# Attention and feed-forward on one core: the second layer's block products regrouped into 512-column steps, its blocks and sums in one tile, and transfers in flight counted by the planner

## The chip, the cores and the metric

One NeuronCore of a Trainium2 chip runs the whole program in one launch. The metric is the device time of one execution in microseconds; lower is better. Engines: TensorE (PE, with PEld for its weight loads), VectorE (DVE), ScalarE (ACT), GpSimd (POOL) and SyncE (SP, which here issues most DMAs).

## The reference

Causal attention with a decay, 8 batches of 8 heads, 576 positions, head size 64; its output, 4608 tokens of 512, goes through two matrix products with a leaky Relu between them. All is float32.

```python
scores = scale * np.matmul(q, k.transpose(0, 1, 3, 2))
cum = np.cumsum(np.log(np.clip(f, 0.0001, 1.0)), axis=-1)
scores = np.where(causal, -1000000000.0, scores + cum[:, :, :, None] - cum[:, :, None, :])
attn = np.exp(scores - np.max(scores, axis=-1, keepdims=True))
attn = attn / (np.sum(attn, axis=-1, keepdims=True) + 1e-09)
x = np.matmul(attn, v).transpose(0, 2, 1, 3).reshape(B * S, H * D)
h = x @ w_in                                       # 512 -> 2048, "first layer"
g = np.maximum(h, 0.0) + alpha * np.minimum(h, 0.0)
return g @ w_out                                   # 2048 -> 512, "second layer"
```

## The kernel before

**Arithmetic.** A float32 product is made of three fast ones: each operand is split into a high part (a copy in the fast format, by ACT) and a low part (the operand less its high part, by DVE or POOL), and high x high, high x low and low x high are added up in PSUM. A PSUM bank is 128 x 512 floats; there are eight.

**Attention and first layer.** 32 pairs of heads follow one another. From pair 9 on (`turned`) the exponentials are turned over by DVE transposes and by 16 small moves a pair of 100 KB (line 920), which SP and POOL issue in turns. The sums' reciprocals go out to DRAM and come back spread over the partitions (`fetch`, lines 657 and 1000); for the last of the first four pairs (`hurry`) `quick` spreads them with six PE products instead. Line 979 or 982 multiplies the attention output by them, 988 and 989 split it. Then the first layer (`ffn1`) can use it: for each of nine token blocks `b` and 16 slices `fc` of its output, twelve matmuls of 512 columns (line 364, `xx` and `wi`) fill one bank. ACT and DVE apply the leaky Relu (lines 1032, 1035, 1037) into one of three buffers `hs`, and SP stores it to DRAM as `hd` (line 1039, 256 KB), from DRAM position [slice][half][partition][token], 512 tokens on end. For the blocks in `LATE` (0, 7 and 8) the Relu is left to the second layer.

**Second layer** (`ffn2`). 18 units of 256 tokens, in the order `UNITS`. The product of a unit is cut into blocks of 128 tokens and 256 outputs, and done with seven block products in place of eight, on sums of blocks (four sums of the tokens' blocks A, four of the weights' blocks B made once in `load_w_out`). The 2048 inputs are taken as eight chunks of two halves, two chunks (`GW`) at a time: a group. For a group, SP loads `hd` into `hr` (line 1252, 512 KB), in late units ACT and DVE apply the Relu (1262, 1267), DVE makes the sums in `gx` (lines 1272 to 1275), ACT makes three pieces of high parts (line 1288) and DVE three of low parts (line 1291) in `gh`. Then PE does, for each of the two chunks, seven products of three matmuls of 256 columns (line 364, `gh` and `wot`): first three of them, then four, into four banks that the unit takes all at once. `PRODS` lists a product's A, its B, its bank and its half of it. After the last group ACT copies one half of bank 3 (line 1314) and DVE adds up the rest in four operations (lines 1318, 1319, 1322, 1323), and SP stores the output (line 1354). The last unit has its own, finer end.

**What sets the order.** Nothing is ordered by hand. Every operation is told to a planner (`Plan`, line 96) with its engine, an estimated duration, a key, the operations that it needs and the buffers that it uses (rings of tiles or banks). `Plan.run` goes through simulated time: of the operations that could start it takes the earliest, with the lower key at a tie, and emits it. So each engine's instructions stand in the planned order, and on the chip each engine works through its own in that order and waits on semaphores. While the plan's time is under 75 us, PE's idle stretches are filled with dummy matmuls (`fill`, line 466). The rings `rhr` (two tiles at first), `rgx` (one) and `rgh` (two) get more tiles when old ones come free: `change3` adds the scratch of the weight sums as four `hr`, `change5` the attention's `xs` as a second `gx`, `change2` the first layer's `xx` as a third `gh` (which the profile names `xx`). `c_mm`, `c_dve` and so on are the durations that the planner believes.

Of the kernel before, what the change touches and what calls it, by code (L numbers as in the profile page):

```python
# [91 lines left out]
ENGS = ("PE", "ACT", "DVE", "POOL", "SP", "-")  # L92


class Plan:
    def __init__(self):
        self.now = dict.fromkeys(ENGS, 0.0)
        self.chan = 0.0
        self.ops = []
        self.banks = self.fill = None  # L100
        self.rnd = random.Random(SEED)
# [27 lines left out]
    def run(self):  # L129
# [76 lines left out]
def attention_moe(  # L206
# [23 lines left out]
    hd = dram.tile([NW, 2, 128, NT], F32, name="hd")  # L230
# [14 lines left out]
    xx = xp.tile([128, 6 * 2 * 512], F32R, name="xx")  # L245
# [11 lines left out]
    hs = xp.tile([128, 7 * 256], F32, name="hs")  # L257
# [29 lines left out]
    xs = xp.tile([128, 2 * S], F32, name="xs")  # L287
    rxs = Ring(Store([xs[:, S * i : S * i + S] for i in range(2)]))
    rri = ring(xp, 1, [128, 4, 6, 32], F32, "ri")
# [6 lines left out]
    tri = sp.tile([128, 128], BF16, name="tri")  # L296
    tri2 = sp.tile([128, 64], BF16, name="tri2")
# [29 lines left out]
    def c_dve(n):  # L327
        return 75 + n / 0.96

# [215 lines left out]
    def attention(n):  # L545
# [4 lines left out]
        hurry = HURRY if n == NP - 1 else 0  # L550

# [75 lines left out]
        def quick(bR, r_, key):  # L627

            bB = [Buf(rT), Buf(rT)]
            at = lambda c0: bB[c0 // 512].t[:, c0 % 512 : c0 % 512 + (128 if c0 < 512 else 64)]  # L630
# [10 lines left out]
            for c0, c1 in ((0, 512), (512, S)):  # L641
                ri_ops.append(op("DVE", c_dve(c1 - c0), lambda c0=c0, c1=c1: ve.tensor_copy(flat(bri)[:, c0:c1], bB[c0 // 512].t[:, 0 : c1 - c0]), key, [q_], [bB[c0 // 512], bri]))

        def quotients(key):
# [8 lines left out]
            if hurry:  # L653
                quick(bR, r_, key)
# [108 lines left out]
        def rest():  # L763
            st = k0 + 11.5 - hurry
# [30 lines left out]
        quotients(k0 + 11 - hurry)  # L795
# [10 lines left out]
    def turned(n):  # L806
# [208 lines left out]
    def ffn1(b):  # L1015

        for fc in range(NF):
# [16 lines left out]
            else:  # L1034
# [5 lines left out]
                hd[fc % NW, fc // NW, :, 512 * b : 512 * b + 512], bs.t), -1000, [cp], [bs], kb=256)  # L1040
# [79 lines left out]
    rhr = ring_later(2, [128, GW, 2, TU], F32, "hr")  # L1120
    rgx = ring_later(1, [128, 4, GW, 128], F32, "gx")
# [20 lines left out]

    def change3():
        st = rhr.store
        for i in range(4):
            st.free.append((plan.t, len(st.items)))
            st.items.append(wx[0].rearrange("p a (b c j) n -> p (a b) c j n", b=2, c=GW)[:, i])

    def change2():
        n = 2 * 7 * GW * 128  # L1150
        st = rgh.store
        for i in range(6 * 2 * 512 // n):
            st.free.append((plan.t, len(st.items)))
            st.items.append(xx[:, n * i : n * i + n].rearrange("p (k j c q) -> p k j c q", k=2, j=7, c=GW))
# [6 lines left out]
    def change5():  # L1161
        rgx.store.free.append((plan.t, len(rgx.store.items)))
        rgx.store.items.append(xs[:, 0:1024].rearrange("p (i c q) -> p i c q", i=4, c=GW))

    o_change = op("-", 0, change, 0, done_a)
    for c in (0, 2):
        bt_ = Buf(rhr)
        tv = lambda bt_=bt_: bt_.t.rearrange("p c j t -> p c (j t)")
        ld = op("SP", 400, lambda c=c, tv=tv: sy.dma_start(tv(), xt[c : c + 2].rearrange("c p t -> p c t")), 1e6, [o_change] + xt_ops, [bt_], kb=512)
        for i in range(2):  # L1170
            bx = Buf(rx)
# [228 lines left out]
```

## Time and profile before

| | |
|---|---|
| median of three runs | 1011.58 us (1008.52 to 1011.61) |
| the profiled execution | 1010.48 us, of which 1008.7 us from its first to its last instruction (the span) |
| busy, share of the span | PE 99%, PE's weight loads 88%, DVE 80%, ACT 60%, POOL 39% |
| chain that ended last | PE 93%, DMA 3%, DVE 2%, ACT, POOL and SP's queue 1% each |
| granted PE clock | full throughout |

The span ends some time before the execution does, so sums are made against the execution's own time. A row of the page gives a group of instructions: line, engine, operation, tiles written and read, shape and number, then the time in which any of them ran, the mean of one, and the idle time of the engine just before. Matmuls overlap in the records (one of 256 columns is shown with 283 ns, but they start more closely), so their pace is read from starts. The stages follow each other: attention with first-layer products in between, the first layer alone from some 550 us, the second layer from 642 us.

### The profile page before, as it was taken

To read this page: it belongs to the slowest core of one execution; us is meant where nothing else is said; L and a number is where in the kernel's file an instruction comes from. 1 tells how busy PE (TensorE), PEld (TensorE's weight loads), DVE (VectorE), ACT (ScalarE), POOL (GpSimd) and SP (SyncE) were. 2 spreads that over 40 slices of the span, in tenths; PEclk is the share of its full clock that TensorE was granted. 3 is DMA by queue.
4 is the path that set the end of the run, shared out by engine and by line. 5 is a ranking of instruction groups with operands and counts; after the bars stand their busy time and mean duration, and the time that the engine had idled before them with its cause. 6 is when DMAs were issued, how large, how long until landed. Compare 5 with 4: busy or idle time off the path is not lost.

```text
span 1008.7 us, 22200 instructions
## 1 busy us (share of the span) xinstructions
PE 999.0 (99%) x7900; PEld 888.5 (88%) x7900; DVE 803.7 (80%) x1745; ACT 606.8 (60%) x1369; POOL 394.6 (39%) x635
## 2 busy tenths in 40 slices
PE   9999999999999999999999999999999999999998
PEld 6778888888888788888888888999999999999998
DVE  7878768888877848868655987788898888989994
ACT  7987876666666645656444766564554645546551
POOL 4575758799988858869740100000000000000000
PEclk9999999999999999999999999999999999999999
DMA  7988748889887887968766666633534344434411
GB/s 225 264 241 245 227 130 230 238 250 264 257 242 211 260 242 206 260 206 233 235 174 241 212 205 212 207 116 123 157 113 142 115 140 132 139 115 137 135 55 42
DMA packets 130686, 191.12 MB, mean 189 GB/s; under 512 B 22088, under 2 KB 79728, under 8 KB 130576
## 3 DMA queue, kind: packets, MB, share of 16 engines
q1 hardware_dynamic: 124400, 170.66, 55.7%
q0 software_dynamic: 5888, 18.85, 7.4%
q8 instruction: 62, 1.02, 0.4%
q14 instruction: 48, 0.39, 0.1%
q10 hardware_dynamic: 288, 0.20, 0.1%
HBM read 102.74 MB, written 48.80 MB: 150 GB/s over the span
## 4 chain that ended last, share of the span: by engine, by line
PE 93%; DMA 3%; DVE 2%; ACT 1%; SPq 1%; POOL 1%; issue 0%; DVEq 0%; ACTq 0%
PE bank L364 89%; PE bank L584 2%; DMA big<-big 1%; SPq L920 1%; DVE big L883 1%; DMA rd<-st 0%; DMA vr<-in_vv_dram 0%; PE bank L432 0%; DMA rqk<-in_qk_dram 0%; ACT big L826 0%; DVE Z L491 0%; PE bank L466 0%; POOL Z L510 0%; ACT big L580 0%; POOL Qhl L538 0%
## 5 line engine op out<-in xcount | busy, mean ns | idle before, releaser
L364 PE MATMUL bank<-xx,wi 128*128 128x512 f32 x1728 | 407.7, 392 | 1.8 <-DVE st L846 1.8
L364 PEld LDWEIGHTS bank<-xx,wi 128*128 128x128 f32 x1728 | 319.8, 188 | 68.4 <-DVE st L846 2.2
L826 ACT ACTIVATE big<-big,st 128x384 f32<-128x384 f32 (+4 forms) x207 | 118.6, 575 | 44.3 <-DVE st L846 44.3
L1037 DVE SCALAR_TENSOR_TENSOR hs<-bank,sa,hs 128x512 f32<-128x512 f32 x96 | 71.2, 743 | 79.0 <-ACT hs L1035 78.8
L364 PE MATMUL bank<-wi,gh 128*128 128x256 f32 x1008 | 123.9, 283 | 0.0
L364 PE MATMUL bank<-wot,gh 128*128 128x256 f32 x1008 | 123.9, 283 | 0.0
L364 PEld LDWEIGHTS bank<-wot,gh 128*128 128x128 f32 x1008 | 122.3, 192 | 0.1
L364 PEld LDWEIGHTS bank<-wi,gh 128*128 128x128 f32 x1008 | 122.3, 192 | 0.0
L1035 ACT ACTIVATE hs<-bank,ab 128x512 f32<-128x512 f32 x96 | 66.1, 689 | 88.3 <-PE bank L364 70.5
L883 DVE STREAM_TRANSPOSE big<-big 128x1408 f32<-128x1408 f32 (+2 forms) x69 | 86.6, 1273 | 22.3 <-DMA hd<-hs 6.7
L364 PEld LDWEIGHTS bank<-big,vr 128*64 128x64 f32 x1884 | 88.9, 137 | 12.0 <-issue 3.9
L364 PE MATMUL bank<-big,vr 128*64 128x128 f32 (+2 forms) x1884 | 95.5, 259 | 2.0 <-DVE st L609 1.1
L538 POOL TENSOR_TENSOR Qhl<-rqk,Qhl 128x640 fp32r<-128x640 f32 (+1 forms) x56 | 83.3, 1496 | 30.8 <-ACT Qhl L537 29.1
L920 POOL DMA_DIRECT2D big<-big x184 | 92.1, 507 | 7.9 <-DVE big L883 4.2
L364 PE MATMUL bank<-Qhl 64*128 64x512 f32 (+6 forms) x840 | 93.1, 326 | 0.1
L364 PEld LDWEIGHTS bank<-Qhl 64*128 64x128 f32 (+1 forms) x840 | 74.9, 186 | 15.8 <-issue 9.1
L510 POOL TENSOR_TENSOR Z<-Z,tri 128x384 f32<-128x384 f32 x60 | 54.6, 922 | 27.9 <-DMA Z<-c 18.5
L364 PE MATMUL bank<-wot,xx 128*128 128x256 f32 x504 | 62.4, 283 | 0.0
L364 PE MATMUL bank<-wi,xx 128*128 128x256 f32 x504 | 62.4, 283 | 0.0
L364 PEld LDWEIGHTS bank<-wi,xx 128*128 128x128 f32 x504 | 61.3, 192 | 0.0
L364 PEld LDWEIGHTS bank<-wot,xx 128*128 128x128 f32 x504 | 61.3, 192 | 0.0
L1032 ACT ACTIVATE hs<-bank,sg 128x512 f32<-128x512 f32 x48 | 33.0, 687 | 33.3 <-PE bank L364 28.4
(176 smaller groups left out, 1501.5 us busy)
## 6 DMA issues: line engine op xcount, KB each, us to landing
hd<-hs SPq DMA_DIRECT2D x144, 256.0 KB, 3.6
wx<-hd SPq DMA_DIRECT2D x46, 512.0 KB, 3.8
big<-big SPq DMA_DIRECT2D x184, 100.0 KB, 5.1
big<-big POOLq DMA_DIRECT2D x184, 100.0 KB, 4.9
rqk<-in_qk_dram SPq DMA_DIRECT2D x28, 608.0 KB, 5.1
hr<-hd SPq DMA_DIRECT2D x26, 512.0 KB, 3.5
vr<-in_vv_dram SPq DMA_DIRECT2D x32, 320.0 KB, 4.4
big<-in_w_in_dram SPq DMA_DIRECT2D x16, 512.0 KB, 6.1
```

The source lines that it names most:

```text
L364: pe.matmul(o, lhsT, rhs, start=start, stop=stop)
L510: m1 = op("POOL", c_po(128 * 3), lambda z4=z4: po.tensor_tensor(z4()[:, 6:9], z4()[:, 0:3], tb(3), ALU.add), kc + 0.1, got + [o_mask], [bZ])
L538: o2 = op("POOL", c_po(w), lambda hi=hi, lo=lo, raw=raw: po.tensor_tensor(lo(), raw(), hi().bitcast(F32), ALU.subtract), kc, [o1], [bqk, bQ])
L584: pe.transpose(t[:, c : c + 128], src[:, 128 * j : 128 * j + 128], ident)
L826: sums.append(op("ACT", c_exp(w), lambda: ac.activation(at(), at(), AF.Exp, bias=lo()[:, col : col + 1], scale=-1.0, accum_out=su()[:, col ...
L883: ve.transpose(t_t[:, :, c0 : c0 + 32 * (b1 - b0)].rearrange("p k (b c) -> p k b c", c=32), bE.t[:, 128 * off : 128 * (off + b1 - b0)].rea ...
L920: moves.append(op(n_, 550 if i % 2 else 450, lambda a=a, k=k, q_=q_: q_.dma_start(bM.t[32 * k : 32 * k + 32, a], t_t[32 * a : 32 * a + 32, ...
L1032: cp = op("ACT", c_act(512), lambda bh=bh, bs=bs, fc=fc: ac.activation(bs.t, bh.t, AF.Copy, scale=sg[:, fc : fc + 1]), -1000, [last, o_sg] ...
L1035: cp = op("ACT", c_act(512), lambda bh=bh, bs=bs, fc=fc: ac.activation(bs.t, bh.t, AF.Relu, scale=ab[:, fc : fc + 1]), -1000, [last, o_sg] ...
L1037: cp = op("DVE", c_dve(512), lambda bh=bh, bs=bs, fc=fc: ve.scalar_tensor_tensor(bs.t, bh.t, sa[:, fc : fc + 1], bs.t, ALU.mult, ALU.add), ...
```

## The change

- **Block products** (17 of 18 units): for the products with the A blocks 0, 2 and 5, one matmul of 512 columns multiplies the high part of A by the high and low parts of B, into the two halves of a bank; then one of 256 columns does low x high into the first half. These three products have banks 3, 2 and (new) 4, five a unit; the others stay. The steps go product by product over both chunks. A step names only its own bank, and each bank is evacuated after its last step. DVE adds the halves of banks 3, 2 and 4 with five adds of 256 columns.
- **One tile** `rhx` (8 KB a partition) holds a group's four blocks and four sums; the sums take one 512-column and two 256-column operations, the high parts two ACT operations, the low parts one DVE operation of 1792 columns. There is one such tile at first, two from `wx`, one from the space of `xx`, one from `hx`, in which `xs`, `ri`, `hs` and the masks now lie. `rhr` and `rgx` are gone.
- **`hd`** is laid out so that a group's load is two runs of 2 KB a partition (four of 1 KB before), and a store four of 512 bytes (one of 2 KB before).
- **The planner** counts transfers in flight: a DMA on SP, POOL or ACT cannot start with 10, 8 or 10 of that queue's in flight. SP's moves are told with 550 in place of 450 ns.
- **Pair 2** too uses `quick`, and its later steps get an earlier key. `quick` uses one bank less.
- Two weight sums change sign, the output's halves of rows change place.

The diff, cut (the last unit's output rows, the pools of scratch tiles and the first layer's ninth block are left out):

```diff
+DEEP = {"SP": 10, "POOL": 8, "ACT": 10}
...
+                    if o.kb and len(self.flying[e]) >= DEEP[e]:
+                        s = max(s, self.flying[e][-DEEP[e]])
...
+                self.flying[o.eng].append(end)
...
-    hd = dram.tile([NW, 2, 128, NT], F32, name="hd")
+    hd = dram.tile([B + 1, NW // GW, 128, 2, 2, 2, GW, 128], F32, name="hd")
...
-    rH, rO = Ring(banks, 2, 4), Ring(banks, 0, 6)
+    rH, rO = Ring(banks, 2, 4), Ring(banks, 0, 8)
...
+    soon = {NP - 1: HURRY, NP - 2: 15}.get(n, 0)
...
-            if hurry:
-                quick(bR, r_, key)
+            if soon:
+                quick(bT, bR, r_, key)
...
-        quotients(k0 + 11 - hurry)
+        quotients(k0 + 11 - soon)
...
-            moves.append(op(n_, 550 if i % 2 else 450, lambda a=a, k=k, q_=q_: q_.dma_start(
+            moves.append(op(n_, 550, lambda a=a, k=k, q_=q_: q_.dma_start(
...
-                hd[fc % NW, fc // NW, :, 512 * b : 512 * b + 512], bs.t), -1000, [cp], [bs], kb=256)
+                hd[b, fc % NW // GW, :, fc // NW, :, :, fc % GW].rearrange("p u i q -> p (u i) q"), bs.t.rearrange("p (k q) -> p k q", q=128)), -1000, [cp], [bs], kb=256)
...
-        bo = [Buf(rO) for _ in range(4)]
+        wide = u != UNITS[-1]
+        bo = dict(zip((3, 2, 4, 1, 0) if wide else (3, 2, 0, 1), [Buf(rO) for _ in range(5 if wide else 4)]))
+        twice = (0, 2, 5) if wide else ()
+        parts = [[PRODS[i] for i in k] for k in ((0,), (1, 5), (3, 4), (2, 6))] if wide else (PRODS[:3], PRODS[3:])
...
-                ve.tensor_tensor(S1, A21, A22, ALU.add)
-                ve.tensor_tensor(S3, A11, A21, ALU.subtract)
-                ve.tensor_tensor(S2, S1, A11, ALU.subtract)
+                A21, A11, A22, A12, S3, S1, S2, S4 = (bhx.t[:, i] for i in range(8))
+                both = bhx.t[:, 0:1].broadcast_to([128, 2, GW, 128])
+                ve.tensor_tensor(bhx.t[:, 4:6], bhx.t[:, 1:3], both, ALU.subtract)
+                ve.tensor_tensor(S2, S1, A11, ALU.add)
                 ve.tensor_tensor(S4, A12, S2, ALU.subtract)
...
+            h0 = op("ACT", c_acs(3 * 128 * GW), lambda bhx=bhx, bgh=bgh: ac.activation(bgh.t[:, 0, 0:3], bhx.t[:, 1:4], AF.Copy), key, o1, [bhx, bgh])
+            o2 = op("DVE", c_tt(256 * GW) + 2 * c_tt(128 * GW), sums, key, o1, [bhx], two=True)
+            h1 = op("ACT", c_acs(4 * 128 * GW), lambda bhx=bhx, bgh=bgh: ac.activation(bgh.t[:, 0, 3:7], bhx.t[:, 4:8], AF.Copy), key, [o2], [bhx, bgh])
+            his, rdy = [h0, h1], [op("DVE", c_tt(7 * 128 * GW), lambda bhx=bhx, bgh=bgh: ve.tensor_tensor(
+                bgh.t[:, 1], bhx.t[:, 1:8], bgh.t[:, 0].bitcast(F32), ALU.subtract), key, [h0, h1], [bhx, bgh], two=True)]
...
+                        if ia in twice:
+                            bank = 4 if ia == 5 else bank
+                            mm(bo[bank].t.rearrange("p (h n) -> p h n", h=2), bgh.t[:, 0, ia, cc], wot[c][:, :, ib], c == 0, False)
+                            mm(bo[bank].t[:, 0:256], bgh.t[:, 1, ia, cc], wot[c][:, 0, ib], False, c == NW - 1)
+                            continue
...
+        def both(i, k):
+            for h, a in ((1, 3), (0, i)):
+                ve.tensor_tensor(bs.t[:, i], bo[k].t[:, 256 * h : 256 * h + 256], bs.t[:, a], ALU.add)
...
-        e1 = op("DVE", 2 * c_dve(512), ends, -500, [e0], bo[:3] + [bs])
-        e2 = op("DVE", c_dve(512) + c_dve(256), ends2, -500, [e1], bo[:2] + [bs])
+        e1 = op("DVE", c_tt(256), lambda: ve.tensor_tensor(bs.t[:, 3], bo[3].t[:, :256], bs.t[:, 3], ALU.add), -500, [e0], [bo[3], bs])
+        for i, k in ((0, 2), (4, 4)):
+            e1 = op("DVE", 2 * c_tt(256), lambda i=i, k=k: both(i, k), -500, [e1, ends_of[-5]], [bo[k], bs])
+        e1 = op("DVE", c_tt(512), ends, -500, [e1, ends_of[-3]], [bo[1], bs])
+        e2 = op("DVE", c_tt(512) + c_tt(256), ends2, -500, [e1, last], [bo[0], bo[1], bs])
```

## Rows read from the trace of the kernel before

**Rows 1.** The page: span, and busy time of each engine.

```profile
span 1008.7 us, 22200 instructions
PE 999.0 (99%) x7900; PEld 888.5 (88%) x7900; DVE 803.7 (80%) x1745; ACT 606.8 (60%) x1369; POOL 394.6 (39%) x635
```

**Rows 2.** Waits of PE, whole run: waiter, releaser, us in total, times, longest.

```profile
PE bank L364 <- DVE st L846: 1.8, 2, 0.9
...
PE bank L364 <- DVE st L609: 1.1, 1, 1.1
PE bank L364 <- DMA rd<-st: 0.8, 1, 0.8
PE bank L584 <- ACT big L580: 0.7, 1, 0.7
PE bank L364 <- DMA vr<-in_vv_dram: 0.2, 1, 0.2
```

**Rows 3.** Second layer by stretch: length, busy (x instructions), granted clock, DMA share, GB/s.

```profile
660.00:985.00 325.00, 325.00 (x2710) 325.00 (x2710) 293.04 (x537) 174.39 (x308) 0.00 (x0) 1.00 0.40 124
```

**Rows 4.** Timeline of PE, 560 to 700 us: start, us, instructions merged.

```profile
559.80 82.44 PE L364 MATMUL bank<-xx,wi 128*128 128x512 f32 x363
...
672.31 10.24 PE L364 MATMUL bank<-wi,gh 128*128 128x256 f32 x84
682.39 5.20 PE L364 MATMUL bank<-wot,xx 128*128 128x256 f32 x42
```

**Rows 5.** Timeline, 640 to 690 us: DVE's operations of one group.

```profile
646.25 0.42 DVE L1272 TENSOR_TENSOR gx<-wx 128x256 f32<-128x256 f32 x1
646.58 0.42 DVE L1273 TENSOR_TENSOR gx<-wx 128x256 f32<-128x256 f32 x1
646.92 0.42 DVE L1274 TENSOR_TENSOR gx<-gx,wx 128x256 f32<-128x256 f32 x1
...
647.37 0.42 DVE L1275 TENSOR_TENSOR gx<-wx,gx 128x256 f32<-128x256 f32 x1
647.72 0.69 DVE L1291 TENSOR_TENSOR gh<-hr,gh 128x512 fp32r<-128x512 f32 x1
648.32 1.22 DVE L1291 TENSOR_TENSOR gh<-xs,gh 128x1024 fp32r<-128x1024 f32 x1
```

**Rows 6.** The Relu's addition (groups by shape), and DVE's largest wait, 660 to 985 us.

```profile
L1267 DVE TENSOR_TENSOR wx<-wx,gx 128x1024 f32<-128x1024 f32 x7 | 8.5, 1220 | 0.0
...
DVE hs L1318 <- ACT xx L1288: 10.6, 5, 2.2
```

**Rows 7.** Timeline, 640 to 690 us: DVE's adds at a unit's end.

```profile
662.13 0.69 DVE L1318 TENSOR_TENSOR hs<-bank,hs 128x512 f32<-128x512 f32 x1 [0.90 <-PE bank L364]
...
662.85 0.69 DVE L1319 TENSOR_TENSOR hs<-bank,hs 128x512 f32<-128x512 f32 x1
663.64 0.69 DVE L1322 TENSOR_TENSOR hs<-bank,hs 128x512 f32<-128x512 f32 x1
664.25 0.41 DVE L1323 TENSOR_TENSOR hs<-bank,hs 128x256 f32<-128x256 f32 x1
```

**Rows 8.** Line 920 (the moves) on SP: issue time min/median/max in ns.

```profile
L920 SPq DMA_DIRECT2D big<-big x184: 507/648/2370, 156.9 to 527.5; - x184
```

**Rows 9.** Timeline, 0 to 60 us: fillers, pair 2's scaling, pair 3's products.

```profile
52.35 1.28 PE L466 MATMUL bank<-big 128*128 128x128 f32 x10
...
56.44 1.43 POOL L979 TENSOR_TENSOR xs<-xs,ri 128x576 f32<-128x576 f32 x1
...
59.91 1.55 PE L364 MATMUL bank<-big,sel 9*128 9x128 f32 x12
```

**Rows 10.** DMA issues (number, KB, us to landing), and ACT's wait for stores.

```profile
hd<-hs SPq DMA_DIRECT2D x144, 256.0 KB, 3.6
...
ri<-rd SPq DMA_DIRECT2D x46, 160.0 KB, 5.2
...
ACT hs L1035 <- DMA hd<-hs: 15.4, 5, 5.4
```

More of the change, by code (lines that the diff above doesn't have):

```diff
@@ L244, in attention_moe @@
     wi = xp.tile([128, NF, 2, NC4, 128], F32R, name="wi")
-    xx = xp.tile([128, 6 * 2 * 512], F32R, name="xx")
+    ctx_x = ExitStack()
+    xx = ctx_x.enter_context(tc.tile_pool(name="xq", bufs=1, side="right")).tile([128, 6 * 2 * 512], F32R, name="xx")
     ctx_a = ExitStack()
@@ L1141, in change, with more @@
         rP.least = 0
+    def more(t):
+        st = rhx.store
+        st.free.append((plan.t, len(st.items)))
+        st.items.append(t.rearrange("p (e c q) -> p e c q", e=8, c=GW))
     def change3():
[L1144 to L1147, printed above, removed]
+        for i in range(2):
+            more(wx[0].rearrange("p a b n -> p a (b n)")[:, i])
     def change2():
-        n = 2 * 7 * GW * 128
         st = rgh.store
-        for i in range(6 * 2 * 512 // n):
-            st.free.append((plan.t, len(st.items)))
-            st.items.append(xx[:, n * i : n * i + n].rearrange("p (k j c q) -> p k j c q", k=2, j=7, c=GW))
+        ctx_x.close()
+        p2 = ctx.enter_context(tc.tile_pool(name="p2", bufs=1, side="right", reuse_waits="tile"))
+        st.free.append((plan.t, len(st.items)))
+        st.items.append(p2.tile([128, 2, 7, GW, 128], F32R, name="gh2"))
+        more(p2.tile([128, 2048], F32, name="hg1"))
         rH.least = 0
@@ L1161, in change5 @@
     def change5():
-        rgx.store.free.append((plan.t, len(rgx.store.items)))
-        rgx.store.items.append(xs[:, 0:1024].rearrange("p (i c q) -> p i c q", i=4, c=GW))
+        more(hx[:, 0:2048])
     o_change = op("-", 0, change, 0, done_a)
[L1166 to L1171, printed above, removed]
-            xh = op("ACT", c_acs(512), lambda i=i, bx=bx, tv=tv: ac.activation(bx.t[:, 0], tv()[:, i], AF.Copy), 1e4, [ld], [bt_, bx])
-            xl = op("DVE", c_dve(512), lambda i=i, bx=bx, tv=tv: ve.tensor_tensor(
-                bx.t[:, 1], tv()[:, i], bx.t[:, 0].bitcast(F32), ALU.subtract), 1e4, [xh], [bt_, bx], two=True)
-            x_ops[B, c + i] = (bx, xh, xl)
+    bt_ = Buf(rhx)
+    tv = lambda: bt_.t.rearrange("p (c e) g q -> p c (e g q)", c=4)
+    ld = [op("SP", 400, lambda c=c: sy.dma_start(tv()[:, c : c + 2], xt[c : c + 2].rearrange("c p t -> p c t")), 1e6, [o_change] + xt_ops, [bt_], kb=512) for c in (0, 2)]
+    for c in range(NC4):
+        bx = Buf(rx)
+        xh = op("ACT", c_acs(512), lambda c=c, bx=bx: ac.activation(bx.t[:, 0], tv()[:, c], AF.Copy), 1e4, [ld[c // 2]], [bt_, bx])
+        xl = op("DVE", c_dve(512), lambda c=c, bx=bx: ve.tensor_tensor(
+            bx.t[:, 1], tv()[:, c], bx.t[:, 0].bitcast(F32), ALU.subtract), 1e4, [xh], [bt_, bx], two=True)
+        x_ops[B, c] = (bx, xh, xl)
     for b in range(B + 1):
@@ L1285, in ffn2 @@
-            o_ = lambda k, j0, j1, bgh=bgh: (bgh.t[:, k, j0] if j1 == j0 + 1 and j0 == 0 else bgh.t[:, k, j0:j1])
-            his, rdy = [], []
-            for j0, j1, src, d, bb in ((0, 1, a_, o1, bhr), (1, 3, b_, o1, bhr), (3, 7, s_(3, 7), o2, bgx)):
-                his.append(op("ACT", c_acs(128 * GW * (j1 - j0)), lambda j0=j0, j1=j1, src=src, o_=o_: ac.activation(
-                    o_(0, j0, j1), src(), AF.Copy), key, [d], [bb, bgh]))
-            for h, (j0, j1, src, bb) in enumerate(((0, 1, a_, bhr), (1, 3, b_, bhr), (3, 7, s_(3, 7), bgx))):
-                rdy.append(op("DVE", c_dve(128 * GW * (j1 - j0)), lambda j0=j0, j1=j1, src=src, o_=o_: ve.tensor_tensor(
-                    o_(1, j0, j1), src(), o_(0, j0, j1).bitcast(F32), ALU.subtract), key, [his[h]], [bb, bgh], two=True))
+                o1 = [op("ACT", 2 * GW * c_acs(TU), acts, key, ld + [o_sg], [bhx])]
@@ L1293, in ffn2 @@
             seen = set()
-            todo = [(cc, part) for cc in range(GW) for part in (PRODS[:3], PRODS[3:])]
+            todo = [(cc, part) for part in parts for cc in range(GW)] if wide else [(cc, part) for cc in range(GW) for part in parts]
             if u == UNITS[-1] and g == NW // GW - 1:
@@ L1304, in prods @@
                             seen.add(bank)
-                            end = c == NW - 1 and n == 2 and (bank == 3 or (ia, bank) in ((6, 0), (4, 1), (5, 2)))
+                            end = c == NW - 1 and n == 2 and (bank == 3 or (ia, bank) in ((6, 0), (3, 1), (5, 2)))
                             mm(o, bgh.t[:, ka, ia, cc], wot[c][:, kb, ib], first, end)
-                last = op("PE", 3 * len(part) * c_mm(256), prods, key + m / 20,
-                          [last] + his + rdy + wo_ready[c], bo + [bgh])
+                last = op("PE", 3 * len(part) * c_mm(256) - 13 * sum(x[0] in twice for x in part), prods, key + m / 20,
+                          [last] + his + rdy + wo_ready[c], [bo[k] for k in bo if k in {4 if wide and x[0] == 5 else x[2] for x in part}] + [bgh])
                 ends_of.append(last)
```

78 lines of the change are left out of this document (36 added, 42 removed).

## The prediction

> **What bounds the kernel now.** I read the page first: TensorE (PE) is busy for 999.0 of 1008.7 us [rows 1]. A busy matmul row may hide waiting, so the PE's waits come next: six in the whole run, 6.0 us together, of which the list shows all but the 1.4 us at the very start [rows 2]; those on the lines 609 and 580 lie near 55 and 65 us, the other three between 231 and 341 us. The table by stage then shows the second layer alone [rows 3]: from 660 to 985 us PE is busy for all of 325.00 us at the full granted clock (1.00, the 2.4 GHz level), without a wait. So there only a change of what PE executes shortens anything, until another engine is slower than PE. The one that is near is VectorE (DVE): 293.04 of 325 us, 90%.
>
> The pace per matmul is read from starts in the timeline, since the durations overlap [rows 4]. 84 matmuls of 256 columns lie between 672.31 and 682.39: 10.08 / 84 = 120.0 ns. 363 matmuls of 512 columns, in the first layer, take 82.44 us: 227 ns each. Twice 120.0 is 240; so one matmul of 512 columns is 13 ns cheaper than two of 256.
>
> **The change part by part.** The profiled execution took 1010.48 us (the span of 1008.7 and 1.8 around it), 1.10 below the median 1011.58 of the three runs; the sum is made against 1010.48.
>
> *512-column steps.* In 17 of 18 units (the last stays as it was), 8 chunks a unit and 3 of 7 products, three 256-column matmuls (3 x 120.0 = 360.0 ns) become one of 512 and one of 256 (227 + 120.0 = 347.0). 17 x 8 x 3 = 408 products x 13.0 ns = **-5.3 us**, all on PE and so on the path. The 512 columns are now two separate runs of 256, the hi and lo parts of one weight block; in the rows they are one run. Bounds are 0 (no cheaper than two of 256) and -5.3. I take -5.3: a 512-column row is nearer to a 512-column step than a 256-column one.
>
> By the Trainium skill, page "TensorE: Matmul & The Clock Gate", section "Wait — 56ns, not 53.3ns?", a warm matmul costs its columns at 2.4 GHz and a fixed part of about 2.5 ns. By that, 408 steps would save an estimated 1.0 us; the starts in rows 4 show a fixed part of 13 ns in this kernel, and the sum goes by them.
>
> *DVE's work for a group of two chunks.* Start to start [rows 5]: two 256-column sums 0.33 and 0.34; a third 0.45 (the next needs its result, which adds 0.12); a fourth 0.35; low parts of 256, 512 and 1024 columns 0.34 (as the sums), 0.60 and 1.13 (0.60 and 512 more columns at (0.60 - 0.33) / 256 = 1.04 ns). Sum 3.54. After the change: a 512-column sum with its reader right behind it 0.72, sums of 0.45 and 0.34, one low part of 1792 columns 1.13 + 0.80 = 1.93: 3.44. That is 0.10 less a group, 0.4 a unit. The 1024-column addition of the groups with Relu, 1.22 in six units, stays [rows 6].
>
> *The unit's end.* Before, four adds [rows 7]: 0.72, 0.79, 0.61 and 0.33 (the last as the sums in rows 5), so 2.45 us. After it three banks hold two halves that must be added first: by the same rows 0.45, 0.45, 0.33, 0.45, 0.45, 0.79, 0.61, 0.33 = 3.86 us. Net for DVE: +1.4 - 0.4 = +1.0 us a unit. A unit has 168 x 0.120 = 20.16 us of PE before and 19.84 after; DVE's mean goes from 0.902 x 20.16 = 18.2 to 19.2 us, 97% of the unit. PE's work still covers it, with 0.6 us left. That cover is the thin point of this change: if it is gone, the price is that of the second rival. I charge 0, bounds 0 and +18.
>
> By the Trainium skill, page "VectorE: DVE Perf Modes", sections "The TRN2 errata — SBUF-src ops pay a fixed extra latency per instruction" and "The DRAIN you can't avoid", an fp32 tensor_tensor costs (N + 151) / 0.96 ns and the next one starts when the pipe is empty. By that (estimate) a group would fall from 4.04 to 3.56 and a unit's end rise from 2.50 to 3.93, half a microsecond less a unit, and the second rival would have no ground. The trace agrees with the duration (0.42 for 256 columns) and not with the wait: independent sums start 0.33 apart in rows 5.
>
> *Banks returned singly.* A unit holds five of eight banks, so its successor can start on three; the fourth that it needs is the first returned. That bank is complete six of eight steps of the last group before the unit's end, about 4 us, and needs one ACT copy and one 0.45 us add. Before, PE had no wait at a unit's end either [rows 3]: 0.
>
> *One tile for blocks and sums.* Raw blocks had six 4 KB buffers and sums two; now five tiles hold both, and a tile is released by the one low part, the last to read it. Five groups are 25 us of PE; load (some 4 us, as the stores of rows 10), sums, ACT copies and low part are some 10. The next load waits on SP for that release, the output stores stand between loads on SP, and the next groups wait for what is behind them: 15 us of cover. The single low part waits for both ACT copies, and in DVE's queue all later work stands behind it; the next group's sums can be placed ahead. While the first layer still runs, the first new tile and the old scratch space serve, two groups as before. 0.
>
> *Counted transfers and the earlier third pair.* [...] This can end at most the 2.8 us of waits after 75 us (1.8, 0.8 and 0.2) [rows 2]; a new order may as well make some. Head pair 2 now gets its reciprocals through PE products, which took 1.55 us for pair 3, and drops four small transfers; its scaling, which started at 56.44, can come earlier. The gain is bounded by filler and waits between 46 and 66 us: 28 filler matmuls in five runs, the longest ten in 1.28 us [rows 9], so 3.1 to 3.6 us, and waits of 1.8. Bounds 1.55 - 3.1 - 1.8 = -3.4 and +1.6. I take **-0.5**, a little to the side of the gain: filler stands only where the plan had nothing ready.
>
> *Stores in 512-byte pieces.* The 144 stores of 256 KB go in four times as many pieces, and the reads in pieces twice as long. No row prices 512 bytes. With equal bytes it is 0; the nearest row with short pieces, 160 KB that land in 5.2 us where a store takes 3.6 [rows 10], makes it up to 1.6 us a store. The evacuation of the first layer waited 15.4 us in five waits for such a store, as its ring has three buffers, without stopping PE; five times 1.6 is 8 us at the worst. I take **+0.5**, by the lower end, since bytes and issues stay as they are.
>
> The pools, the sign of the weight sums, the output's row order and the numbering of the products keep the instruction counts: 0. Sum: -5.3 - 0.5 + 0.5 = -5.3, so 1005.2; forecast **1005 us**, 0.65% below the median. About 0.3%, 3 us, is what a measurement can tell from no change.
>
> **The rivals.**
>
> *First: given back before 640 us.* Finer stores and a new order on SP and POOL make PE wait 3 to 8 us more. For it: the moves fill SP's queue [rows 8], and three store buffers were already waited for [rows 10]. Against it: while such waits last, the planner has first-layer products to put in. 1005 + 3 to 8 = 1008 to 1013, mostly no change that can be told.
>
> *Second: DVE becomes the bound of the second layer, slower.* The place is the unit's end and the units with Relu. DVE's waits between 660 and 985 us sum to 27.1 us, the largest 10.6 [rows 6], 1.7 a unit. If they stay beside 19.2 us of work, a unit takes 20.9 in place of 19.84, and 17 units 18 us more: 1023. It decides from 0.6 us of waits a unit on. Against it: most of this waiting is behind PE, for buffers that it frees, and goes when DVE is late.
>
> *Third: the saving is not there.* A step of two runs costs what two steps of 256 columns cost, and 1010 stays: no change. Nothing in rows 4 shows a cost of starting a run without a new matmul. By the page on TensorE above it would be 1009.5.
>
> *Fourth: more than the products.* The early start removes the filler and the waits too: 1000 to 1002. For it: 28 fillers. Against it: a new order seldom removes all waits.
>
> **How the numbers follow.** Forecast 0.60, first rival 0.16, second 0.12, third 0.04, fourth 0.08. Faster by over 0.3% (below 1008.5): forecast and fourth, 0.68. Within 0.3%: first and third, 0.20. Slower: second, 0.12. The range reaches from the fourth's 1000 to the first's 1013 and leaves the second out.
>
> **What would show it.** Right: in the second layer PE is busy throughout, 19.84 us a unit, with 512-column steps 227 ns apart; DVE is at 97%; the second layer is 5 us shorter, and the first ends within 2 us of the 642 us of before. Wrong: an idle PE in the second layer, released by DVE's low parts or adds (second); the first layer ending 4 us later, PE waiting for transfers (first); steps 240 ns apart (third). Over 1013 us with no gap on PE in the second layer would refute the whole account.

## The result, and the profile after

The changed kernel takes **1021.66 us** (median of 6 runs, 1020.89 to 1024.71) where the kernel before takes 1011.60 (6 runs): ratio 1.0097, 95% interval 1.0075 to 1.0119. It is 1% slower; the forecast was 1005, and the range ended at 1013. The profiled execution took 1021.5, 11.0 more than that of before.

The second layer did nearly what was forecast. Its stretch by itself, to be held against [rows 3] (columns as there):

```profile
680.00:980.00 300.00, 300.00 (x2177) 283.81 (x2177) 284.53 (x382) 149.90 (x226) 0.00 (x0) 1.00 0.42 133
```

PE is busy for all of 300 us at the full granted clock, and DVE has gone from 90% to 95% (284.53 of 300). PE's timeline, which answers to [rows 4]:

```profile
574.74 83.23 PE L374 MATMUL bank<-xx,wi 128*128 128x512 f32 x356
657.80 10.16 PE L374 MATMUL bank<-wot,gh 128*128 128x512 f32 x72
667.80 10.07 PE L374 MATMUL bank<-wi,gh 128*128 128x512 f32 x72
677.71 10.12 PE L374 MATMUL bank<-wot,gh 128*128 128x512 f32 x72
```

Two rows of 72 matmuls make a unit: 657.80 to 677.71, 19.91 us, where 168 matmuls took 20.16. From its first matmul to the start of the last, the layer takes 357.8 us (657.80 to 1015.63) where it took 362.8: **4.9 us less**.

The starts in the trace tell where these 4.9 us come from. A step of 512 columns takes 233.9 ns on average, not the 227 of the forecast, and the 256-column step behind it 117.6: 351.5 ns a product, 8.5 less than 360, which makes 3.5 us over 408 products. The other 1.4 us come from the 256-column steps of the products that were left alone, 119.2 ns in place of 120.0. Both repeat with a period of three groups, and there are three tiles `gh`, which hold the stationary operand: a product takes 347.7, 353.5 and 353.3 ns in the three, a step left alone 119.5, 119.9 and 118.2.

But it begins at 657.80 where it began at 642.08, and these 15.7 us are the result. The first of the rows above has one cause in it: 356 first-layer matmuls in 657.80 - 574.74 = 83.06 us are 233.3 ns each, where 363 of them took 227. Their code, shapes and number are those of before. The same in one stretch of 55 us, before and after:

```profile
575.00:630.00 55.00, 55.00 (x244) 45.57 (x243) 44.97 (x82) 36.22 (x55) 0.00 (x0) 1.00 0.67 217
```

```profile
575.00:630.00 55.00, 55.00 (x237) 44.20 (x236) 46.71 (x79) 35.68 (x52) 0.00 (x0) 1.00 0.79 233
```

After (the second fence), PE does 237 matmuls in place of 244 at the same clock of 1.00 and without a gap; and the DMA engines are busy 0.79 of the time for 233 GB/s, where they needed 0.67 for 217. Per GB/s that is 0.34% against 0.31%.

PE's waits in the whole run, against [rows 2]:

```profile
PE bank L374 <- DMA rd<-st: 4.0, 2, 2.6
PE bank L374 <- DVE st L620: 2.0, 1, 2.0
PE bank L442 <- DVE big L439: 1.4, 1, 1.4
PE bank L374 <- POOL xx L1000: 0.3, 1, 0.3
```

They are 7.7 us in place of 6.0, so no list of waits shows the 15.7. But the longest has something behind it, in the stretches around it:

```profile
210.00:220.00 10.00, 7.88 (x49) 6.16 (x47) 6.15 (x14) 5.98 (x15) 8.98 (x15) 1.00 0.88 228
220.00:230.00 10.00, 9.57 (x84) 8.75 (x85) 6.98 (x18) 4.22 (x14) 5.35 (x12) 0.83 0.91 227
```

PE is idle for 2.1 us, and in the next 10 us its granted clock is 0.83: a third of the time at the lower of its two levels, 1.2 GHz, which costs 1.7 us more. Before, these stretches had no idle PE and a clock of 1.00:

```profile
210.00:220.00 10.00, 10.00 (x92) 8.24 (x92) 7.23 (x16) 5.44 (x13) 9.48 (x14) 1.00 0.89 242
220.00:230.00 10.00, 10.00 (x76) 8.33 (x74) 9.12 (x25) 9.31 (x26) 9.74 (x19) 1.00 0.98 263
```

The stores (DMA issues) and ACT's waits for them, against [rows 10]:

```profile
hd<-hx SPq DMA_DIRECT2D x144, 256.0 KB, 4.1
```

```profile
ACT hx L1046 <- DMA hd<-hx: 29.9, 12, 5.6
```

A store lands in 4.1 us where it took 3.6, and ACT's waits for them went from 15.4 us to 29.9. Adding up PE's time from start to start in the trace, by kind of matmul, up to the second layer (us; a wait, or a lower clock, counts with the matmul in front of it or in it; some runs of the next section beside):

| | before | after | after_64 | second_only | so_512 |
|---|---|---|---|---|---|
| first layer (1728) | 401.3 | 410.2 | 403.6 | 401.0 | 408.4 |
| attention (3094) | 232.9 | 237.0 | 236.8 | 231.9 | 236.0 |
| fillers | 5.0 | 6.2 | 6.2 | 5.2 | 5.0 |
| reciprocals' products | 1.5 | 3.0 | 3.0 | 1.5 | 1.5 |
| second layer begins at | 642.1 | 657.8 | 651.0 | 641.0 | 652.2 |

### The profile page after: what moved, and what is told of

Read it like the earlier page. It is cut to its first block, busy times and chain, and to the rows that moved or that the text cites. A ratio compares the mean times of both kernels' runs of the same rounds, so it can differ in the third digit from the quotient of the medians.

```text
span 1019.7 us, 21116 instructions
## 1 busy us (share of the span) xinstructions
PE 1008.0 (99%) x7512; PEld 869.8 (85%) x7512; DVE 814.6 (80%) x1599; ACT 593.3 (58%) x1297; POOL 395.0 (39%) x635
## 4 chain that ended last, share of the span: by engine, by line
PE 86%; DMA 8%; DVE 3%; SPq 2%; issue 1%; ACT 1%; POOL 0%; DVEq 0%; ACTq 0%
PE bank L374 82%; DMA big<-big 5%; PE bank L595 2%; DMA hd<-hx 2%; SPq L931 1%; DVE big L894 1%; DMA rd<-st 1%; PE bank L442 1%; PE bank L476 0%; DVE big L857 0%; ACT hx L1046 0%; DVE Z L501 0%; POOL xx L1000 0%; DMA vr<-in_vv_dram 0%; DVE hx L1048 0%
## 5 line engine op out<-in xcount | busy, mean ns | idle before, releaser
L374 PE MATMUL bank<-wot,gh 128*128 128x256 f32 (+1 forms) x1308 | 181.9, 300 | 0.0
L374 PE MATMUL bank<-wi,gh 128*128 128x256 f32 (+1 forms) x1308 | 181.9, 300 | 0.0
L374 PEld LDWEIGHTS bank<-wot,gh 128*128 128x128 f32 x1308 | 171.2, 190 | 9.3
L374 PEld LDWEIGHTS bank<-wi,gh 128*128 128x128 f32 x1308 | 171.1, 190 | 9.2
L1048 DVE SCALAR_TENSOR_TENSOR hx<-bank,sa,hx 128x512 f32<-128x512 f32 x96 | 70.7, 741 | 73.5 <-ACT hx L1046 73.2
L1046 ACT ACTIVATE hx<-bank,ab 128x512 f32<-128x512 f32 x96 | 65.7, 686 | 88.4 <-PE bank L374 57.4
L374 PEld LDWEIGHTS bank<-Qhl 64*128 64x128 f32 (+1 forms) x840 | 75.3, 186 | 15.4 <-issue 4.0
L520 POOL TENSOR_TENSOR Z<-Z,hx 128x384 f32<-128x384 f32 x60 | 54.7, 922 | 28.4 <-DMA Z<-c 19.3
L1296 DVE TENSOR_TENSOR gh<-hg,gh 128x1792 fp32r<-128x1792 f32 x28 | 56.5, 2018 | 1.2 <-ACT gh L1295 1.2
L1296 DVE TENSOR_TENSOR gh<-wx,gh 128x1792 fp32r<-128x1792 f32 x28 | 56.2, 2017 | 0.0
L1000 POOL TENSOR_TENSOR xx<-hx,xx 128x512 fp32r<-128x512 f32 x32 | 42.0, 1320 | 35.0 <-ACT xx L999 31.3
```

The source lines that it names most:

```text
L374: pe.matmul(o, lhsT, rhs, start=start, stop=stop)
L520: m1 = op("POOL", c_po(128 * 3), lambda z4=z4: po.tensor_tensor(z4()[:, 6:9], z4()[:, 0:3], tb(3), ALU.add), kc + 0.1, got + [o_mask], [bZ])
L1000: xl = op("POOL", c_po(512), lambda: po.tensor_tensor(bx.t[:, 1], bxs.t[:, 0:512], bx.t[:, 0].bitcast(F32), ALU.subtract), st, [xh], [bxs, ...
L1046: cp = op("ACT", c_act(512), lambda bh=bh, bs=bs, fc=fc: ac.activation(bs.t, bh.t, AF.Relu, scale=ab[:, fc : fc + 1]), -1000, [last, o_sg] ...
L1048: cp = op("DVE", c_dve(512), lambda bh=bh, bs=bs, fc=fc: ve.scalar_tensor_tensor(bs.t, bh.t, sa[:, fc : fc + 1], bs.t, ALU.mult, ALU.add), ...
L1296: his, rdy = [h0, h1], [op("DVE", c_tt(7 * 128 * GW), lambda bhx=bhx, bgh=bgh: ve.tensor_tensor(bgh.t[:, 1], bhx.t[:, 1:8], bgh.t[:, 0].bi ...
```

## The experiments

**1. The address of the moving tile.** The change puts the tile xx, whose 512 columns every first-layer matmul reads, in a pool at the right end of SBUF. There it begins at byte 204768 of a partition, 32 past a multiple of 64; before it began at 67008, a multiple of 64. Two kernels move it in the kernel before and change nothing else.

```diff
-    xx = xp.tile([128, 6 * 2 * 512], F32R, name="xx")
+    xx = ctx.enter_context(tc.tile_pool(name="xq", bufs=1, side="right")).tile([128, 6 * 2 * 512], F32R, name="xx")   # before_r32
+    ... .tile([128, 6 * 2 * 512 + 8], F32R, name="xx")   # before_r64: eight floats longer, begins at 204736
```

> The kernel before, its order of instructions unchanged; only the tile xx, the moving operand of the first layer, lies at the right end of the partition, as in the changed kernel: byte 204768, which is 32 past a multiple of 64 (before: 67008, a multiple of 64). Theory A (the offset within 64 bytes makes a 512-column matmul 6.7 ns longer, as the changed kernel's 233.3 ns against 226.7): 1728 of them, up to 11.5 us more, less what waits already covered: 1020 to 1023 us. Rival B (the place, the far end of the memory, costs it): the same 1020 to 1023 us here, but also in the next kernel. Rival C (the pace of the changed kernel comes from its stores, queues or order, not from where xx lies): 1011.6 us and 226.7 ns a step, unchanged.

> As the kernel with xx at the right end, but the tile is 32 bytes longer, so that it starts at byte 204736, a multiple of 64. Theory A: 226.7 ns a step and 1011.6 us, as before. Rival B (place): 233 ns and 1020 to 1023 us. Rival C: 1011.6 us.

before_r32: 1017.82 us, ratio 1.0077 (1.0051 to 1.0102). before_r64: 1010.96, ratio 0.9998 (0.9984 to 1.0013). PE's timeline of the one and of the other:

```profile
574.72 75.06 PE L364 MATMUL bank<-xx,wi 128*128 128x512 f32 x321
649.62 10.24 PE L364 MATMUL bank<-wot,gh 128*128 128x256 f32 x84
```

```profile
574.74 68.62 PE L364 MATMUL bank<-xx,wi 128*128 128x512 f32 x302
643.20 10.23 PE L364 MATMUL bank<-wot,gh 128*128 128x256 f32 x84
```

(649.62 - 574.72) / 321 = 233.3 ns, and (643.20 - 574.74) / 302 = 226.7. The place at the right end costs nothing, the 32 bytes cost 6.7 ns a matmul. The whole grew less than theory A said (1020 to 1023): of the 11.5 us that 1728 times 6.7 ns would be, 6.4 show. So the same eight floats go into the changed kernel (after_64), and, in a second run, sixteen, of which the tile leaves out the first twelve, so that it begins 16 past a multiple of 64 (after_16).

> The changed kernel, its order of instructions unchanged, with xx 32 bytes earlier, at a multiple of 64. Theory A: the first layer's steps fall from 233.3 to 226.7 ns, 1728 of them are 11.5 us, of which 9 to 11.5 show: 1010 to 1013 us in place of 1021.7; the second layer keeps its 357.8 us. Rivals B and C: 1021 to 1022 us, 233 ns a step.

> The changed kernel with xx at a byte that is 16 past a multiple of 64. Theory A, if a 2 KB row that starts anywhere inside a 64-byte line touches one line more: 233.3 ns a step, 1021 to 1022 us. If only the 32-byte half counts (16 past is like a multiple of 64): 226.7 ns and 1010 to 1013 us. If the cost grows with the distance: some 230 ns, about 1016 us.

after_64: 1015.73, ratio 1.0053 (1.0029 to 1.0077), 5.9 below the change as it is; its first layer takes 403.6 us, no longer 410.2. The 226.7 ns of theory A came, its 1010 to 1013 us did not. after_16, one run: 1019.32, 408.0 us of first layer and 231.7 ns a matmul, between the 230 and the 233.3 that were expected for two of three guesses. Some 6 of the 10 us are settled; after_64 is still slower than before, with a second layer that is 4.9 us shorter.

**2. The parts that touch the first stage, undone.** Three are left: the stores in 512-byte pieces (S), the counted transfers with the moves booked at 550 ns (C), and pair 2 scaled by matmuls (Q). Each alone is taken out of after_64, and then all three (second_only, which has the second layer of the change and nothing else of it).

```diff
-    hd = dram.tile([B + 1, NW // GW, 128, 2, 2, 2, GW, 128], F32, name="hd")      # S
+    hd = dram.tile([B + 1, NW, 128, 2, 512], F32, name="hd")                      # stores in 2-KB pieces
-DEEP = {"SP": 10, "POOL": 8, "ACT": 10}                                            # C
+DEEP = {"SP": 10**6, "POOL": 10**6, "ACT": 10**6}                                  # and 450 ns on SP again
-        soon = {NP - 1: HURRY, NP - 2: 15}.get(n, 0)                               # Q
+        soon = {NP - 1: HURRY}.get(n, 0)
```

> The second layer as changed, with xx at a multiple of 64 bytes; stores in pieces of 2 KB as before (a group's load is then two transfers of 512-byte pieces), no counting of transfers (450 ns for SP's moves again), pair 2 by way of DRAM as before. Theory: the 7.8 us by which the first stage is still longer with the aligned tile (651.0 against 643.2 us) come from these three, and none from the second layer's edit. Then the first stage ends at 641 to 645 us, the second layer takes 358 us as in the changed kernel, and the whole 1004 to 1009 us: below both kernels. Rival: the shared tile hx, or any change of the planner's random draws, costs as much; then the first stage ends at 648 us or later and the whole is 1012 us or more.

> The changed kernel with xx at a multiple of 64 bytes and stores of 2 KB pieces as before (loads in 512-byte pieces); counting and pair 2 as changed. Theory S (the 512-byte pieces load the DMA engines: share 0.75 against 0.67 in the first layer alone, at the same GB/s): most of the 7.8 us come back, first stage at 643 to 646 us, whole 1007 to 1011. Theory P (the counted order) or Q (pair 2): the first stage stays at 649 to 651 us, whole 1014 to 1016.

> The changed kernel with xx at a multiple of 64 bytes, without the count of transfers and with 450 ns for SP's moves again. Theory P: first stage at 643 to 646 us, whole 1007 to 1011. Theories S and Q: 649 to 651 and 1014 to 1016 us.

> The changed kernel with xx at a multiple of 64 bytes, pair 2 by way of DRAM as before. Theory Q (1.5 us of PE products, 1.2 us more of fillers, and what the shift costs): first stage at 646 to 649 us, whole 1010 to 1013. Theories S and P: at most the 1.5 us of the products come back: 649 to 650 us, 1013 to 1015.

store_2k 1014.33 (ratio 1.0023, 1.0007 to 1.0040), no_count 1013.39 (1.0014, 0.9994 to 1.0033), no_quick2 1018.32 (1.0062, 1.0035 to 1.0089): one alone gives back 2.3 us at most, and without Q it is 2.6 us slower. None of the three by itself makes up most of the loss: the second layer begins at 648.7 in store_2k, 650.2 in no_count and 653.7 in no_quick2 (651.0 in after_64). second_only: **1007.22, ratio 0.9957 (0.9934 to 0.9980)**, below both kernels. Its second layer begins at 641.0 and takes 357.8 us, as expected. So the three together cost 8.5 us, and their shares don't add up by undoing one at a time.

**3. Each part alone added to second_only, and a seed.** This gives the other four of the eight combinations (so_count, so_quick2, so_512 have one part; the three runs above have two), and so_seed67 changes only the planner's random seed, so as to see what a new order costs by itself.

```diff
-SEED = 66
+SEED = 67
```

> The run second_only with the planner's random seed 67 instead of 66: the same instructions in another order. If the order of before is one lucky draw and each new order costs (theory L), the second layer's first matmul goes from 641.0 to 646 to 655 us and the total from 1007 to 1012 to 1020. If the three first-stage parts of the change cost by themselves (theory P), an order from another seed costs nothing of the kind: start 639 to 643, total 1005 to 1010.

> The run second_only with pair 2 scaled by matmuls again, as in the change (12 more quick matmuls, 1.5 us of PE). Theory P, with the three parts adding up: undoing this part alone in after_64 cost 2.7 us of start, so putting it in alone should give 0 to 3 us back, start 638 to 642.5. Theory L: any new order costs 4 to 14 us, start 645 to 655.

> The run second_only with the transfers in flight counted (10, 8, 10) and the table moves booked at 550 ns on SP as well. Theory P: it costs 1 to 6 us (attention matmuls 237 instead of 232 us of PE time, since no_count alone gave 4.7 us of attention back), start 642 to 647. Theory L: start anywhere from 645 to 655, with the first layer's matmuls as likely to carry it as attention's.

> The run second_only with the stores of the hidden layer in 512-byte pieces and the loads in 2-KB pieces, as in the change. The order of the instructions hardly changes, since the planner books a store by its bytes. Theory P: the stores cost 2 to 4 us by slower transfers in the first layer, whose matmuls take 402 to 404 us where second_only has 401.0; start 643 to 645. If the transfers' pieces cost nothing by themselves: start 640 to 642.5.

Medians in us of the eight (5 to 10 runs each; the kernel before beside them took 1011.4 to 1012.4):

| | no S | S |
|---|---|---|
| neither C nor Q | 1007.22 (second_only) | 1017.35 (so_512) |
| Q | 1010.07 (so_quick2) | 1013.39 (no_count) |
| C | 1012.35 (so_count) | 1018.32 (no_quick2) |
| C and Q | 1014.33 (store_2k) | 1015.73 (after_64) |

In each of the four rows S costs: 10.1, 3.3, 6.0 and 1.4, mean **5.2 us**. C, compared in the same way, costs 5.1, 4.3, 1.0 and 2.3, mean **3.2 us**. Q is +2.9, -4.0, +2.0 and -2.6: mean -0.4, nothing. so_seed67 takes 1011.23 (0.9992, 0.9979 to 1.0005), 4.0 above second_only: an order alone does that. The second layer begins at 647.8 in so_seed67 and at 650.1 in so_count, as theory L had it, and at 643.8 in so_quick2, between both; so_512, with 652.2, is above both of its ranges. Whether the order of the kernel before is a favourable one is open: it was not run with another seed.

so_512 is the clear one. It has second_only's order of PE instructions, and is 10.1 us slower. PE's waits in second_only, then in so_512, and the mean granted clock of so_512:

```profile
PE bank L374 <- DVE st L620: 1.8, 1, 1.8
PE bank L442 <- DVE big L439: 1.4, 1, 1.4
PE bank L374 <- DVE hx L1048: 1.3, 1, 1.3
PE bank L374 <- DMA hd<-hx: 0.6, 1, 0.6
```

```profile
PE bank L374 <- DMA hx<-rd: 3.4, 1, 3.4
PE bank L374 <- DVE hx L1048: 3.1, 3, 1.3
PE bank L374 <- DMA rd<-st: 2.0, 1, 2.0
PE bank L374 <- DVE st L620: 1.8, 1, 1.8
PE bank L442 <- DVE big L439: 1.4, 1, 1.4
PE bank L374 <- issue: 0.4, 1, 0.4
```

```profile
core 0: 1013.9 us, clock 0.995
```

The chain of so_512 that ended last (start, us, what), around the wait of 3.4 us and around two for L1048, the second half of an evacuation:

```profile
193.15 9.53 DMA big<-big
...
202.74 2.47 DMA hx<-rd
...
205.22 9.96 PE bank L374 x85
```

```profile
434.40 4.47 DMA hd<-hx
...
439.00 1.14 ACT xx L999 x2
440.13 0.59 ACT hx L1046
...
440.75 0.76 DVE hx L1048
...
441.55 10.46 PE bank L374 x85
```

In the first a move and then a small transfer land late, and attention stands. In the second the store itself is late: SP issued it at 434.40, behind moves of which one had waited 2.7 us for an earlier store, and it took 4.47 us; its buffer is the one that ACT writes next, so a bank is not emptied, and PE's timeline shows who wanted it, products of attention:

```profile
439.94 0.44 PE L374 MATMUL bank<-Qhl 64*128 64x384 f32 x1 [1.26 <-DVE hx L1048]
441.55 2.55 PE L374 MATMUL bank<-Qhl 64*128 64x384 f32 x17 [1.18 <-DVE hx L1048]
```

What the two do to the clock, in so_512's stretches and in the same ones of second_only:

```profile
200.00:210.00 10.00, 6.56 (x69) 5.87 (x68) 4.82 (x10) 2.07 (x5) 4.82 (x8) 0.83 0.70 213
...
440.00:450.00 10.00, 8.82 (x48) 7.01 (x50) 4.32 (x15) 5.02 (x12) 9.77 (x16) 0.66 0.87 256
```

```profile
200.00:210.00 10.00, 9.42 (x92) 8.06 (x91) 7.07 (x18) 4.31 (x14) 7.29 (x14) 1.00 0.83 258
...
440.00:450.00 10.00, 10.00 (x126) 8.83 (x120) 7.51 (x17) 5.81 (x15) 7.18 (x12) 1.00 0.72 218
```

The waits are 3.4 us at the one place and 1.3 + 1.2 at the other; the lower clock behind them, (1 - 0.83) x 10 and (1 - 0.66) x 10, costs another 1.7 and 3.4. Over so_512's whole span the granted clock is 0.995: 5 us, half of its loss. PE's waits are 12.1 us in place of 5.1; so 7.0 of waits and 5 of clock stand against 11.2 us by which the second layer begins later (652.2 against 641.0). The same shows between executions of second_only: four with a clock of 1.000 took 1003.4 to 1006.2, mean 1005.0; four with 0.998 took 1007.2 to 1013.7, mean 1009.9, where 0.002 of the time is 2.0 us.

**4. The pieces by halves, and each part under the other seed.** so_1k stores in pieces of 1 KB, with second_only's order of instructions on every engine. so_512_67 and so_count67 are so_seed67 with S and with C.

```diff
-    hd = dram.tile([B + 1, NW, 128, 2, 512], F32, name="hd")
+    hd = dram.tile([B + 1, NW, 128, 2, 2, 256], F32, name="hd")   # so_1k
```

> The run second_only with the stores of the hidden layer in 1-KB pieces; the order of the instructions on every engine is that of second_only (1007.2 us, 2-KB pieces) and, in the first stage, of so_512 (1017.35 us, 512-byte pieces). If the price of the stores is that of their pieces, it lies between: 1008 to 1013 us, second layer from 642 to 648. If any disturbance of the timing costs the same by chance, it is anywhere from 1005 to 1018, and more likely at 1014 or more than at 1009. If a piece of 512 bytes is below some size and one of 1 KB is not: 1006 to 1009.

> The run so_seed67 (1011.2 us, second layer from 647.8) with the stores in 512-byte pieces; the first stage's order on PE is that of so_seed67. If the stores cost by themselves: 3 to 10 us more, 1014 to 1021. If the 10 us of so_512 belong to the order of seed 66: 1008 to 1013.

> The run so_seed67 (1011.2 us) with the transfers in flight counted and the table moves booked at 550 ns on SP. If the counting makes worse orders by itself, 3 to 5 us more: 1014 to 1017. If an order is a draw, whatever makes it, this is a fresh draw between 1007 and 1017, as likely below 1011 as above.

so_1k: 1012.56 (1.0007, 0.9988 to 1.0026). In one order of instructions, 2-KB, 1-KB and 512-byte pieces take 1007.2, 1012.6 and 1017.4 us. S also makes the loads' pieces longer (2 KB in place of 512 bytes); so_1k does not (its loads stay in packets of 512 bytes), so its 5.3 us go with the stores alone. The DMA share and GB/s of 575 to 630 us, in that order:

```profile
575.00:630.00 55.00, 55.00 (x244) 45.53 (x244) 46.60 (x76) 35.06 (x53) 0.00 (x0) 1.00 0.61 204
```

```profile
575.00:630.00 55.00, 55.00 (x245) 45.53 (x244) 47.72 (x80) 35.24 (x52) 0.00 (x0) 1.00 0.72 224
```

```profile
575.00:630.00 55.00, 55.00 (x244) 45.55 (x243) 47.66 (x78) 35.51 (x53) 0.00 (x0) 1.00 0.71 213
```

0.61 / 204, 0.72 / 224 and 0.71 / 213 are 0.299, 0.321 and 0.333% of the engines' time per GB/s. Packet by packet in the same stretch, a piece of 2 KB takes 86 ns at the median, one of 1 KB 47 and one of 512 bytes 27: 43, 47 and 54 ns per KB. The Trainium skill, page "DMA: Bandwidth & Descriptors", section "Specifications", puts the smallest transfer at line rate at 512 bytes; by that neither size would cost anything, and these shares and packets disagree.

so_512_67: 1013.73 (1.0010, 0.9995 to 1.0025), 2.5 above so_seed67; the two intervals overlap, so under this seed the price of S is 2.5 with much doubt. so_count67: 1009.37 (0.9967, 0.9945 to 0.9987), 1.9 **below** so_seed67. So counting has no price of its own that survives a change of seed: it makes another order, and a new order was worth +4.0 us in so_seed67, +5.1 in so_count and -1.9 here. S cost 10.1 us in one order, clear of the noise, and 2.5 in the other, not clear of it; that the order decides how much of a late store is covered fits this, and is not shown.

**5. One run for the wide step.** The step of 512 columns in the second layer takes 234 ns, where the first layer's takes 227. so_run puts hi and lo parts of a weight block side by side.

```diff
-            wot[i] = p1.tile([128, 2, 7, 256], F32R, name=f"wot{i}")
+            wot[i] = p1.tile([128, 7, 2, 256], F32R, name=f"wot{i}").rearrange("p j k n -> p k j n")
```

> The run second_only with the halves of each weight block side by side, so that a 512-column step of the second layer reads one run of 2 KB in place of two of 1 KB, 7 KB apart; the order of PE's instructions is the same. If the two runs are what makes that step 233.9 ns where the first layer's is 226.7 ns: 7 ns x 408 steps = 2.9 us less in the second layer, 355.0 instead of 357.8, total 1004.3. If its price is that of the change of weights: no difference, 357.6 to 358, total 1007.

```profile
680.00:980.00 300.00, 300.00 (x2178) 283.80 (x2177) 284.37 (x385) 146.40 (x215) 0.00 (x0) 1.00 0.43 129
```

2178 matmuls in 300 us, as in second_only, and a second layer of 357.8 us; 1009.42 us in all (0.9968, 0.9945 to 0.9992), within second_only's spread. The two runs are not it. The 7 ns go with the group, as shown above: in every third one a product takes 347.7 ns, close to the forecast 347.0, in the others 353.4. No run of the changed kernel places these tiles otherwise, so the cause stays open.

## Why the prediction was wrong

**512-column steps, -5.3 us: near in the sum, in part by luck.** The second layer is 4.9 us shorter, 3.5 of them from the products that were regrouped (8.5 ns each, forecast 13.0) and 1.4 from 256-column steps that the forecast took as unchanged. The sign of being right, 512-column steps 227 ns apart, did not come; they are 233.9. second_only's total is 5.2 below the kernel before beside it (1007.22 against 1012.43); that this total agrees so well is in part the order's doing, since so_seed67, the same change in another order, is 1.0 below (1011.23 against 1012.25). The third rival is out. So is the 1.0 us that follows from the fixed part in the Trainium skill's page "TensorE: Matmul & The Clock Gate".

**DVE, unit ends, banks, the one tile, 0: right.** DVE rose to 95%, forecast 97%; PE never waits there (300.00 of 300 us busy). The parts, from the DVE groups of the changed kernel between 680 and 980 us:

```profile
L1296 DVE TENSOR_TENSOR gh<-hg,gh 128x1792 fp32r<-128x1792 f32 x24 | 48.4, 2017 | 0.0
...
L1329 DVE TENSOR_TENSOR hx<-bank,hx 128x256 f32<-128x256 f32 x60 | 24.1, 422 | 2.8 <-PE bank L374 1.2
```

The low part lasts 2.02 us, and 1.94 from start to start (706.92 to 708.86 us), forecast 1.93. The half microsecond less a unit that follows from the Trainium skill's page "VectorE: DVE Perf Modes" did not come: DVE's busy share rose. The section "The DRAIN you can't avoid" itself says that an operation which is not held starts earlier, and the estimate left that out. The second rival did not come. What the prediction said against it, that most of DVE's waiting before was behind PE, is not what the list of waits says: of the 27.1 us it puts 22.2 to ACT and 4.5 to PE. Its point of decision was not put to a test.

**"The pools ... keep the instruction counts: 0": the step that failed first.** It is the term that was put at nothing, and it measured 5.9 us. A pool sets an address, and an address 32 bytes past a multiple of 64 costs 6.7 ns of every first-layer matmul that PE issues back to back: 5.9 us in the change, 6.4 in the kernel before. No row of before could price it, since its one tile of this use lay at a multiple of 64; but the only reason given for the 0, that the instruction counts stay, says nothing of an address.

**Stores, +0.5 of 0 to 8: the second step that failed, the wrong end.** The mechanism was in the bounds, five waits for a store of the ring of three; ACT's 15.4 us became 29.9. Taken alone it cost 10.1, on average over the four combinations 5.2 us. "Bytes and issues stay as they are" was no reason: the engines' time per byte didn't stay (27 ns for 512 bytes, 86 for 2 KB). The bound of 8 missed what comes on top, the lower clock behind each longer wait, and that moves and small transfers of attention are late too.

**Counting and pair 2, -0.5 of -3.4 to +1.6: wrong.** The fillers did not go; they went from 5.0 to 6.2 us, and the products cost 1.5 us more. Pair 2 comes to nothing on average. The orders that counting brought under one seed cost 3.2 us on average, twice the upper bound, since the waits that a new order may make were named and not priced; a fresh seed shows 4.0 us for such a price. The cover named against the first rival, that the planner puts first-layer products into such waits, did not hold: PE's order is fixed by the plan, and stores that land late, up to 8.7 us after their issue in so_512, stop PE where it stands.

So the first rival, "given back before 640 us" by 3 to 8, is what happened, with 8.5 us, just above its range, and mostly by its mechanism: in the profiled execution of after_64 PE's waits are 10.6 us, where those of second_only are 5.1, and the reciprocals' products and fillers take 2.5 us more, together 8.0 of the 10.0 us between the starts of the second layer. The 5.9 us of the address, of which no rival spoke, come on top; without them the kernel would still be slower than before and above the range (after_64, 1015.73). -5.2 + 8.5 + 5.9 = +9.2; measured +10.0. These are differences of runs that follow on each other, so they add up by construction; the 0.8 is that the kernel before took 1012.43 beside second_only and 1011.60 beside the change. The prediction's last sentence applies: over 1013 us with no gap on PE in the second layer, the account as a whole was refuted, though its largest term stands in the main.

## What to carry to other kernels

When a change moves a tile, compare its address with the old one before anything else, and keep a matmul's moving operand at a multiple of 64 bytes. In a kernel that PE fills, a list of PE's waits shows only part of a loss: add the lower clock behind each wait, and count the time per matmul of code that nobody touched. A change of a planned kernel brings a new order with it; price that order by another seed (4.0 us here) before the change is blamed or praised, and change a layout in memory in one order of instructions.

## What was not expected of the hardware

A 512-column matmul of fp32r data runs at 226.7 ns where its moving operand begins at a multiple of 64 bytes, 231.7 at 16 bytes past one (a single run) and 233.3 at 32. At 2.4 GHz the last is 16 cycles more. The stationary operand doesn't follow: in before_r32 the second layer's steps whose stationary operand lies in the shifted tile are faster (42 of them from 659.69 to 664.65, 118.1 ns each, where the others take 120), and that layer takes 360.8 us in place of 362.8.

```profile
659.69 5.13 PE L364 MATMUL bank<-wi,xx 128*128 128x256 f32 x42
664.65 5.20 PE L364 MATMUL bank<-wi,gh 128*128 128x256 f32 x42
```

It takes little to lower the clock, and the same wait does it at one time and not at another. Two waits of 1.3 and 1.2 us were followed by 0.66 in so_512. In the stretch from 50 to 60 us, so_run and second_only have the same wait of 1.75 us (10.00 - 8.25 of idle PE), at a clock of 0.85 and of 1.00:

```profile
50.00:60.00 10.00, 8.25 (x85) 7.79 (x84) 8.38 (x23) 6.48 (x19) 7.16 (x6) 0.85 0.94 282
```

```profile
50.00:60.00 10.00, 8.25 (x103) 7.53 (x101) 8.91 (x27) 7.46 (x21) 6.89 (x7) 1.00 0.93 279
```

What decides between the two is not in these rows.
